# Moving the MLP gradients of an attention backward kernel behind head 29, with their rows in a K/V slot

## The chip, the cores and the metric

The kernel runs on one core of a Trainium2 chip. The metric is the device time of one execution in microseconds (us), given as the median of several runs. The engines are called TensorE (PE in the profile), VectorE (DVE), ScalarE (ACT), GpSimd (POOL) and SyncE (SP; SPq for its queue of instructions). GpSimd and SyncE do little here but issue DMAs.

## The reference

It is one decode step of a transformer block (one token, 32 heads with 8192 cached keys and values of width 128, a gated MLP of width 1728) together with all its gradients:

```python
def _fwd_reference(A_x, A_k_cache, A_v_cache, A_wq, A_wo, B_x, B_w1, B_w3, B_w2):
    # _A_ref: q = x@wq; p = softmax(q k^T * Dh**-0.5); o = p v; o @ wo
    # _B_ref: h = silu(x@w1) * (x@w3); h @ w2
    x = A_x
    xn = _layernorm(x, axis=-1)
    return x + _A_ref(xn, ...) + _B_ref(xn, B_w1, B_w3, B_w2)

def reference(..., grad_out):
    _out, _vjp = jax.vjp(_f, A_x, A_k_cache, A_v_cache, A_wq, A_wo, B_w1, B_w3, B_w2)
    return (_out, *_vjp(grad_out))
```

The gradients of K and V are outer products, one per head, each as large as the cache that was read: a head loads 4.2 MB and stores 4.2 MB. The gradients of W1, W3 and W2 are outer products too, 6.6 MB in all. Their inputs are known early, so they can be written at any time. The change is about when.

## The kernel before

All K and V tiles, and the large gradient tiles, take turns in nine slots of 2 MB. A new tile gets the slot that is released next, and whoever touches it first waits for the slot's last user, which is mostly a store that has to land.

```python
    kvpool = ctx.enter_context(tc.tile_pool(name="kv", bufs=9))
    def kv_tile(nm):
        return kvpool.tile([P, KVN], BF16, name=nm, tag="kv")
    def load_kv(n):                        # in the order K0, V0, K1, V1, ...
        for h, w in kv_seq[kv_next[0]:kv_next[0] + n]:
            t = kv_tile("Vt" if w else "Kt")
            nc.sync.dma_start(t[:], (vc if w else kc)[h])
            kv_tiles[h, w] = t
        kv_next[0] += n
```

A head has three parts. `phase_a(h)` transposes K on TensorE in eight pieces, each copied out by ScalarE (`KT`), makes the scores, and does the softmax (VectorE: `mrow`, `gmax`, `negM`; ScalarE: `E`). `phase_t(h)` makes the gradient of the softmax from V (VectorE: `T`, `negD`, `U`; TensorE sums `T` into `dp`). `phase_b(h)` overwrites V and K by their gradients on VectorE and stores them. Each engine runs its instructions in the order of the program that the compiler made; an instruction that waits holds everything behind it on its engine (ScalarE stands 12.13 us in this way in after, and 17.11 us in e5, both shown below).

The MLP gradients need two "broadcast rows", vectors of 1728 elements repeated on all 128 partitions. They are made by a chain between ScalarE and TensorE:

```python
    def make_bc(wi, bc, on_act):
        for b0 in range(0, NB, 4):                      # four steps for a row
            dg = small.tile([P, 4, P], BF16, name="dgm", tag="dg", bufs=1)
            ... nc.scalar.activation(dg[:, k, :], ident_bf[:], ACTF.Copy, scale=dgu[...])
            pb = pst_f()
            nc.tensor.matmul(pb[:, 0:bn * P], lhsT=ones_bf[:], rhs=dg[...], ...)
            nc.scalar.copy(bc[:, f0:f1], pb[:, 0:f1 - f0])   # L420 in the profile
        return bc

    def grads_bc(wi):                                   # into a spare weight buffer
        t = wpool.tile([P, NC * GW], BF16, name="bc_t", tag=("wo_g", "wq_g")[wi], bufs=3)
        gt["bc", wi] = make_bc(wi, t, True)

    def grads_w(wi):                                    # gradient of W1, W3
        t = kv_tile("oW")
        ...
        if wi == 0:
            gt["C"] = kv_tile("oC")
        ...                                             # 5 multiplies on VectorE, 2 stores
    def grads_w2():                                     # gradient of W2
        t = kv_tile("oD")
        ...                                             # 14 multiplies on VectorE, 3 stores
```

The main loop (H is 32):

```python
    for h in range(2, H):
        ...
        if h == H - 6:
            grads_bc(0)
            grads_bc(1)
        if h + 1 < H:
            phase_a(h + 1)
            phase_t(h + 1)
        ...
        phase_b(h)
        if h == H - 6:
            grads_w(0)
        elif h == H - 5:
            grads_w(1)
        elif h == H - 4:
            grads_w2()
        load_kv(2)
```

So in the kernel before, three gradient tiles enter the rotation ahead of the last loads: `oW` and `oC` before V30 and K31, and the second `oW` before V31. `oD` comes after all loads.

Of the kernel before, what the change touches and what calls it, by code (L numbers as in the profile page):

```python
# [9 lines left out]
BF16 = mybir.dt.bfloat16  # L10
F32 = mybir.dt.float32
ALU = mybir.AluOpType
# [4 lines left out]
P = 128  # L17
# [4 lines left out]
def kernel(  # L22
# [22 lines left out]
    nc = tc.nc  # L45
    H = A_k_cache.shape[1]
    SK = A_k_cache.shape[2]
    DH = A_k_cache.shape[3]
    D = A_x.shape[2]
    F = B_w1.shape[1]  # L50
    assert DH == P and D % P == 0 and SK % P == 0
    NC = D // P
# [3 lines left out]
    GW = GH * DH  # L56
    KVN = J * DH
# [4 lines left out]
    wpool = ctx.enter_context(tc.tile_pool(name="wp", bufs=2))  # L62
# [9 lines left out]
    dkc = out_2.rearrange("b h (p j) d -> (b h) p (j d)", p=P)  # L72
    dvc = out_3.rearrange("b h (p j) d -> (b h) p (j d)", p=P)
# [12 lines left out]
    g_bc = consts.tile([P, D], BF16, name="g_bc")  # L86
    nc.scalar.dma_start(g_bc[:], grad_out.rearrange("a b d -> (a b d)").partition_broadcast(P))

    NB = (F + P - 1) // P
    NFULL = F // P  # L90
    RB = F - NFULL * P
    NBA = 12
    NA = NC - 1

    def kv_tile(nm):
        return kvpool.tile([P, KVN], BF16, name=nm, tag="kv")
# [12 lines left out]
    def load_group(g):  # L109
        wq_g = wpool.tile([P, NC, GW], BF16, name="wq_g", tag="wq_g", bufs=3)  # L110
        nc.sync.dma_start(wq_g[:], wq_v[:, :, g * GW:(g + 1) * GW])
        wo_g = wpool.tile([P, GH, D], BF16, name="wo_g", tag="wo_g", bufs=3)
        nc.sync.dma_start(wo_g[:], wo_v[:, g * GH:(g + 1) * GH, :])
        grp[g] = dict(wq=wq_g, wo=wo_g)
# [5 lines left out]
    def load_kv(n):  # L120
# [5 lines that stand above are left out]
# [49 lines left out]
    def pst_f():  # L175
        return ps_t.tile([P, 512], F32, name="pF", tag="pT")
# [7 lines left out]
    xn_col = consts.tile([P, NC], F32, name="xn_col")  # L184
# [147 lines left out]
    def outer(dst, vec, pair, lo, hi):  # L332
        n = hi - lo
        nc.vector.tensor_tensor(  # L334
            dst[:, lo * DH:hi * DH].rearrange("p (j a b) -> p j a b", a=DH // 2, b=2),
            vec.rearrange("p (a b) -> p a b", b=2).unsqueeze(1).to_broadcast([P, n, DH // 2, 2]),
            pair[:, lo:hi, :].unsqueeze(2).to_broadcast([P, n, DH // 2, 2]), ALU.mult)

    def phase_b(h):
        g, hh = divmod(h, GH)  # L340
        G_ = grp[g]
        qh = G_["qs"][:, hh, :]
        doh = G_["do"][:, hh, :]
        Vt = kv_tiles.pop((h, 1))
        Kt = kv_tiles.pop((h, 0))
        S_ = hd.pop(h)
        P2, U2 = S_["P2"], S_["U2"]
        for lo in range(0, J, J // 2):
            outer(Vt, doh, P2, lo, lo + J // 2)
        (nc.sync if h >= H - 2 else nc.gpsimd).dma_start(dvc[h], Vt[:])  # L350
        for lo in range(0, J, J // 2):
            outer(Kt, qh, U2, lo, lo + J // 2)
        (nc.sync if h >= H - 2 else nc.gpsimd).dma_start(dkc[h], Kt[:])  # L353

    def finish_group(g):
        G_ = grp[g]
# [45 lines left out]
    def make_bc(wi, bc, on_act):  # L402
        id2 = ident_bf[:].rearrange("p (a b) -> p a b", b=2)
        for b0 in range(0, NB, 4):
            bn = min(4, NB - b0)
            dg = small.tile([P, 4, P], BF16, name="dgm", tag="dg", bufs=1)
            if on_act:
                for k in range(bn):
                    nc.scalar.activation(dg[:, k, :], ident_bf[:], ACTF.Copy, scale=dgu[:, wi, b0 + k:b0 + k + 1])
            else:  # L410
                nc.vector.tensor_tensor(dg[:, 0:bn].rearrange("p k (a b) -> p k a b", b=2),
                                        id2.unsqueeze(1).to_broadcast([P, bn, P // 2, 2]),
                                        dgu2[:, wi, b0:b0 + bn, :].unsqueeze(2).to_broadcast([P, bn, P // 2, 2]),
                                        ALU.mult)
            pb = pst_f()
            nc.tensor.matmul(pb[:, 0:bn * P], lhsT=ones_bf[:],
                             rhs=dg[:, 0:bn].rearrange("p k a -> p (k a)"), start=True, stop=True)
            f0 = b0 * P
            f1 = min(F, f0 + bn * P)
            nc.scalar.copy(bc[:, f0:f1], pb[:, 0:f1 - f0])  # L420
        return bc

    hcol = consts.tile([P, NB], F32, name="hcol")
# [67 lines left out]
                                     start=False, stop=True, skip_group_check=True)  # L491

    gt = {}

    def grads_bc(wi):
        t = wpool.tile([P, NC * GW], BF16, name="bc_t", tag=("wo_g", "wq_g")[wi], bufs=3)
        gt["bc", wi] = make_bc(wi, t, True)

    def grads_w(wi):
        t = kv_tile("oW")  # L500
        v = t[:, 0:NA * F].rearrange("p (c f) -> p c f", f=F)
        bc = gt["bc", wi]
        if wi == 0:
            gt["C"] = kv_tile("oC")
        tb = gt["C"][:, wi * F:(wi + 1) * F]
        dv = (dw1_v, dw3_v)[wi]
        for ci in range(NA):
            nc.vector.tensor_scalar(v[:, ci, :], bc[:, 0:F], xn_col[:, ci:ci + 1], None, ALU.mult)
        nc.gpsimd.dma_start(dv[:, 0:NA, :], v)
        nc.vector.tensor_scalar(tb, bc[:, 0:F], xn_col[:, NA:NC], None, ALU.mult)  # L510
        nc.gpsimd.dma_start(dv[:, NA, :], tb)

    def grads_w2():
        t = kv_tile("oD")
        d2a = t[:, 0:NBA * D].rearrange("p (b c) -> p b c", c=D)
        d2b = gt["C"][:, 2 * F:2 * F + (NB - NBA) * D].rearrange("p (b c) -> p b c", c=D)
        for b in range(NBA, NB):
            nc.vector.tensor_scalar(d2b[:, b - NBA, :], g_bc[:], hcol[:, b:b + 1], None, ALU.mult)
        nc.gpsimd.dma_start(out_8[NBA * P:NFULL * P, :].rearrange("(fb p) c -> p fb c", p=P),
                            d2b[:, 0:NFULL - NBA, :])  # L520
        if RB:
            nc.gpsimd.dma_start(out_8[NFULL * P:F, :], d2b[0:RB, NFULL - NBA, :])
        for b in range(NBA):
            nc.vector.tensor_scalar(d2a[:, b, :], g_bc[:], hcol[:, b:b + 1], None, ALU.mult)
        nc.gpsimd.dma_start(out_8[0:NBA * P, :].rearrange("(fb p) c -> p fb c", p=P), d2a)


    prep_group(0)
    for h in range(2):
        phase_a(h)  # L530
        phase_t(h)
        phase_b(h)
        load_kv(2)
        if h == 0:
            load_group(1)
# [4 lines left out]
    for h in range(2, H):  # L540
        g, hh = divmod(h, GH)
        if hh == 1 and g + 1 < NG:
            load_group(g + 1)
        if hh == GH - 1 and g + 1 < NG:
            prep_group(g + 1)
        if h == H - 6:
            grads_bc(0)
            grads_bc(1)
        if h + 1 < H:
            phase_a(h + 1)  # L550
            phase_t(h + 1)
        if h == H - 1:
            finish_group(g)
        phase_b(h)
        if h == H - 6:
            grads_w(0)
        elif h == H - 5:
            grads_w(1)
        elif h == H - 4:
            grads_w2()  # L560
        load_kv(2)
        if hh == GH - 1 and h < H - 1:
            finish_group(g)
# [58 lines left out]
```

## Time and profile before

| | |
|---|---|
| time, median of 4 runs in the comparison | 753.07 us (751.85 to 754.21) |
| bytes moved, mean rate in the profiled run | 304.35 MB, 405 GB/s |
| TensorE, VectorE busy | 592.9 us (79%), 549.3 us (73%) |
| mean granted TensorE clock | 0.776 |
| last K/V load issued | 691.46 us |
| head 31's scores complete (`mrow`) | 712.76 us |

The first view is three lines of the page: the span in 40 slices of 18.8 us, with the DMA's busy share in tenths and its rate, and the packet counts.

```profile
DMA  8999999999999999999999999999999999799978
GB/s 343 388 425 430 412 427 413 419 419 381 424 421 423 419 412 411 417 421 416 427 430 424 427 423 430 425 414 420 421 433 384 394 363 428 294 356 424 412 299 345
DMA packets 35051, 304.35 MB, mean 405 GB/s; under 512 B 2840, under 2 KB 13912, under 8 KB 18568
```

The rate drops from about 420 GB/s to 294 and 356 in slices 35 and 36, and to 299 in slice 39. The next view reads these stretches in windows of 10 us. Its columns are the busy time of each engine (number of instructions), the granted TensorE clock, the DMA share and the rate.

```profile
core 0: us, PE busy (x) PEld busy (x) DVE busy (x) ACT busy (x) POOL busy (x), PEclk, DMA share, GB/s
640.00:650.00 10.00, 4.09 (x99) 4.09 (x99) 5.07 (x8) 1.59 (x3) 0.76 (x1) 0.50 0.75 319
650.00:660.00 10.00, 7.72 (x81) 5.98 (x79) 7.70 (x9) 2.92 (x5) 1.08 (x2) 0.80 0.62 223
...
720.00:730.00 10.00, 2.79 (x77) 2.39 (x75) 9.26 (x12) 0.00 (x0) 0.00 (x0) 0.78 0.47 197
```

There are two holes: 640 to 660 us (319 and 223 GB/s), and 720 to 730 us (197 GB/s). The first is explained by the queue of SyncE, which issues the loads. This is the line for the gradient tiles in the list of what it waited for between 560 us and the end (us in total, times, longest; the other lines are cut).

```profile
SPq L123 <- DMA out_dram<-oW: 40.8, 2, 22.8
```

SyncE stood 40.8 us, in two waits, for the gradient tiles' own stores (`oW`) to land before it could load into their slots. These are the last three loads in SyncE's timeline (start, duration, engine, line, operation):

```profile
658.48 0.33 SPq L123 DMA_DIRECT2D Vt<-in_A_v_cache_dram  x1
672.95 0.33 SPq L123 DMA_DIRECT2D Kt<-in_A_k_cache_dram  x1
691.46 0.33 SPq L123 DMA_DIRECT2D Vt<-in_A_v_cache_dram  x1
```

These are V30, K31 and V31; the two waits end at V30 and V31. K31 follows 14.5 us after V30 without a wait for `oW`. VectorE met the same slots from the other side, as its timeline shows; in brackets is its idle time before the instruction and what ended it.

```profile
644.93 0.67 DVE L508 TENSOR_SCALAR oW<-bc_t,xn_col 128x1728 bf16<-128x1728 bf16 x1 [11.11 <-DMA out_dram<-Vt]
645.51 0.34 DVE L324 SCALAR_TENSOR_TENSOR U<-DP,negD,P 128x128 bf16<-128x128 f32 x1
```

VectorE stood 11.11 us at the first `oW` multiply for a Vt store, and head 27's `U`, on which its K store depends, stood behind it.

The broadcast rows are visible in ScalarE's timeline at head 26:

```profile
597.50 0.59 ACT L420 CAST bc_t<-pF 128x512 bf16<-128x512 f32 x1 [2.90 <-PE sA L319]
...
617.23 1.01 ACT L265 COPY KT<-pT 128x1024 bf16<-128x1024 bf16 x1 [0.53 <-PE pT L261]
```

From 597.5 to 617.2 us ScalarE copies no `KT`: the chain of eight row copies (L420), of which the first is shown with the `KT` copy that follows the last, keeps the place.

### The profile page before, as it was taken

The numbers are of one execution on the slowest core, as the hardware profiler recorded it, in microseconds if no ns is written. First come the engines' busy times: TensorE is split into PE (matmuls) and PEld (weight loads), VectorE is DVE, ScalarE is ACT, GpSimd is POOL, SyncE is SP. The second block draws the span as 40 slices with busy tenths as digits, with TensorE's granted clock in tenths as the row PEclk, the third lists the DMA queues.
The fourth block names the chain that finished last, engine by engine and source line by source line (L and its number), as shares of the span: only waits on it lengthen the run. The fifth ranks groups of instructions, "written<-read, shape, count | busy, mean of one in ns | idle before, by whom it ended". The sixth has DMA issues, their size and how long they took to land.

```text
span 751.9 us, 23383 instructions
## 1 busy us (share of the span) xinstructions
PE 592.9 (79%) x10618; PEld 506.5 (67%) x10637; DVE 549.3 (73%) x802; ACT 331.1 (44%) x480; POOL 52.3 (7%) x91
## 2 busy tenths in 40 slices
PE   5978899898869868799768994799637978679852
PEld 3855687887668757787667873688527857568741
DVE  1787777787779738986788674986549793588895
ACT  3801555544528414554427451455504666236401
POOL 0000000100001000100001000100001000011101
PEclk9965998798769859797759696797856958668665
DMA  8999999999999999999999999999999999799978
GB/s 343 388 425 430 412 427 413 419 419 381 424 421 423 419 412 411 417 421 416 427 430 424 427 423 430 425 414 420 421 433 384 394 363 428 294 356 424 412 299 345
DMA packets 35051, 304.35 MB, mean 405 GB/s; under 512 B 2840, under 2 KB 13912, under 8 KB 18568
## 3 DMA queue, kind: packets, MB, share of 16 engines
q1 hardware_dynamic: 22404, 159.74, 52.0%
q0 software_dynamic: 12384, 142.96, 45.4%
q8 instruction: 83, 1.36, 0.7%
q10 hardware_dynamic: 164, 0.17, 0.1%
q14 instruction: 16, 0.13, 0.0%
HBM read 151.51 MB, written 151.34 MB: 403 GB/s over the span
## 4 chain that ended last, share of the span: by engine, by line
issue 43%; PE 23%; DMA 10%; DVE 7%; POOL 3%; ACT 2%; POOLq 0%; SPq 0%; ACTq 0%
PE dp L308 6%; PE pT L261 6%; DMA wo_g<-in_A_wo_dram 4%; DVE Kt L334 4%; DMA out_dram<-Vt 3%; DMA wq_g<-in_A_wq_dram 3%; PE sA L327 2%; PE sA L290 2%; PE sA L268 2%; ACT KT L265 2%; DVE Vt L334 1%; POOL out_dram L353 1%; POOL out_dram L350 1%; PE pT L381 1%; PE acc L490 1%
## 5 line engine op out<-in xcount | busy, mean ns | idle before, releaser
L265 ACT COPY KT<-pT 128x1024 bf16<-128x1024 bf16 x256 | 243.6, 1038 | 53.9 <-PE pT L261 52.7
L308 PE MATMUL dp<-T,ident_bf 128*128 128x256 bf16 x1024 | 182.0, 312 | 32.4 <-DVE T L306 31.1
L306 DVE TENSOR_TENSOR T<-Vt,do_g 128x2048 bf16<-128x2048 bf16 x128 | 154.2, 1214 | 51.5 <-DMA Vt<-in_A_v_cache_dram 43.9
L261 PE MATMUL pT<-ident_bf,Kt 128*128 128x128 bf16 x2048 | 174.3, 236 | 1.7 <-issue 1.5
L334 DVE TENSOR_TENSOR Vt<-do_g,P 128x4096 bf16<-128x4096 bf16 x64 | 146.0, 2282 | 3.6 <-PE sA L290 3.6
L334 DVE TENSOR_TENSOR Kt<-qs_g,U 128x4096 bf16<-128x4096 bf16 x64 | 145.5, 2279 | 2.0 <-PE sA L327 1.9
L261 PEld LDWEIGHTS <-Kt 128*128 128x128 bf16 x2048 | 138.0, 107 | 6.3 <-issue 3.5
L308 PEld LDWEIGHTS <-ident_bf 128*128 128x128 bf16 x1024 | 103.2, 111 | 57.3 <-issue 36.3
L268 PEld LDWEIGHTS <-KT 128*128 128x128 bf16 x2048 | 81.8, 99 | 33.8 <-ACT KT L265 23.5
L268 PE MATMUL sA<-qc_g,KT 128*128 128x1 bf16 x2048 | 90.4, 165 | 15.3 <-ACT KT L265 8.2
L327 PE MATMUL sA<-U,Kt 128*128 128x1 bf16 x2048 | 58.4, 164 | 33.2 <-DVE U L324 31.7
L327 PEld LDWEIGHTS <-Kt 128*128 128x128 bf16 x2048 | 58.7, 101 | 35.1 <-issue 34.5
L290 PEld LDWEIGHTS <-Vt 128*128 128x128 bf16 x2048 | 56.7, 97 | 19.7 <-issue 18.4
L290 PE MATMUL sA<-P,Vt 128*128 128x1 bf16 x2048 | 56.5, 164 | 13.8 <-DVE P L287 13.6
L329 ACT COPY od_g<-sA 128x2 f32<-128x2 f32 x32 | 5.1, 160 | 129.1 <-PE sA L327 94.9
L281 ACT ACTIVATE E<-sA,negM 128x64 f32<-128x64 f32 x32 | 10.4, 325 | 100.9 <-DVE negM L278 100.9
L350 POOL DMA_DIRECT2D out_dram<-Vt x30 | 16.4, 548 | 407.8 <-DVE junk L318 228.3
L235 ACT COPY KT<-pT 128x1024 bf16<-128x1024 bf16 (+1 forms) x24 | 20.0, 874 | 33.4 <-PE pT L233 33.2
L353 POOL DMA_DIRECT2D out_dram<-Kt x30 | 16.3, 545 | 167.0 <-DVE U L324 63.9
L274 DVE TENSOR_REDUCE gmax<-sA 1x1 f32<-1x128 f32 x32 | 8.8, 276 | 22.0 <-PE sA L272 21.8
L271 DVE TENSOR_REDUCE mrow<-sA 128x1 f32<-128x64 f32 x32 | 7.1, 221 | 24.2 <-PE sA L268 23.9
L312 DVE TENSOR_REDUCE DP<-dp 128x64 f32<-128x256 f32 x32 | 13.3, 415 | 14.5 <-PE dp L308 14.5
(144 smaller groups left out, 488.2 us busy)
## 6 DMA issues: line engine op xcount, KB each, us to landing
Kt<-in_A_k_cache_dram SPq DMA_DIRECT2D x32, 2048.0 KB, 17.8
Vt<-in_A_v_cache_dram SPq DMA_DIRECT2D x32, 2048.0 KB, 24.4
out_dram<-Vt POOLq DMA_DIRECT2D x30, 2048.0 KB, 15.1
out_dram<-Kt POOLq DMA_DIRECT2D x30, 2048.0 KB, 19.9
wq_g<-in_A_wq_dram SPq DMA_DIRECT2D x8, 640.0 KB, 24.6
wo_g<-in_A_wo_dram SPq DMA_DIRECT2D x8, 640.0 KB, 25.4
out_dram<-wo_g POOLq DMA_DIRECT2D x8, 640.0 KB, 20.4
out_dram<-wq_g POOLq DMA_DIRECT2D x8, 640.0 KB, 23.8
```

What stands on the lines that cost most here:

```text
L235: nc.scalar.copy(wT[:, 0:len(bl), :], pT[:, 0:len(bl), :])
L261: ins = nc.tensor.transpose(pT[:, k, :], K3[:, 8 * c + k, :], ident_bf[:])
L265: nc.scalar.copy(KT[:], pT[:])
L268: nc.tensor.matmul(sA[:, j:j + 1], lhsT=KT[:, k, :], rhs=qcol, start=(j == 0), stop=True, skip_group_check=True)
L290: nc.tensor.matmul(sA[:, OC:OC + 1], lhsT=V3[:, j, :], rhs=P2[:, j, 0:1], start=False, stop=(j == J - 1), skip_group_check=True)
L306: nc.vector.tensor_tensor(T3, V3[:, :, ds_], do_h[:, ds_].unsqueeze(1).to_broadcast([P, J, QD]), ALU.mult)
L308: ins = nc.tensor.matmul(dp[:], lhsT=ident_bf[:], rhs=T3[:, :, R * i:R * (i + 1)], start=(q == 0 and i == 0), stop=(q == DH // QD - 1 and ...
L312: nc.vector.tensor_reduce(DP[:], dp[:], AX.X, ALU.add)
L327: nc.tensor.matmul(sA[:, OC + 1:OC + 2], lhsT=K3[:, j, :], rhs=U2[:, j, 0:1], start=False, stop=(j == J - 1), skip_group_check=True)
L334: nc.vector.tensor_tensor(dst[:, lo * DH:hi * DH].rearrange("p (j a b) -> p j a b", a=DH // 2, b=2), vec.rearrange("p (a b) -> p a b", b=2 ...
L350: (nc.sync if h >= H - 2 else nc.gpsimd).dma_start(dvc[h], Vt[:])
L353: (nc.sync if h >= H - 2 else nc.gpsimd).dma_start(dkc[h], Kt[:])
```

## The change

The intent was to let the last loads go ahead of all gradient tiles, and to make and store the gradients next to head 29's outer products, where the DMA would otherwise run out of work. The rows move from spare weight buffers into a third K/V slot (`oC`), the W2 gradient into weight buffers, and the gradient stores from GpSimd's queue to SyncE's. Head 30's own two stores go the other way, from SyncE to GpSimd.

```diff
-        (nc.sync if h >= H - 2 else nc.gpsimd).dma_start(dvc[h], Vt[:])
+        (nc.sync if h >= H - 1 else nc.gpsimd).dma_start(dvc[h], Vt[:])
 ... (the same for dkc)
-    def grads_bc(wi):
-        t = wpool.tile([P, NC * GW], BF16, name="bc_t", tag=("wo_g", "wq_g")[wi], bufs=3)
-        gt["bc", wi] = make_bc(wi, t, True)
+    CB = 2 * F + (NB - NBA) * D
 ...
+    def grads_bc():
+        gt["C"] = kv_tile("oC")
+        for wi in range(2):
+            gt["bc", wi] = make_bc(wi, gt["C"][:, CB + wi * F:CB + (wi + 1) * F], True)
 ... (grads_w: nc.gpsimd.dma_start -> nc.sync.dma_start)
     def grads_w2():
-        t = kv_tile("oD")
 ...
+        for i, b0 in enumerate(range(0, NBA, 4)):
+            t = wpool.tile([P, 4, D], BF16, name="oD", tag=("wo_g", "wq_g")[i % 2], bufs=3)
+            for k in range(4):
+                nc.vector.tensor_scalar(t[:, k, :], g_bc[:], hcol[:, b0 + k:b0 + k + 1], None, ALU.mult)
+            nc.sync.dma_start(out_8[b0 * P:(b0 + 4) * P, :].rearrange("(fb p) c -> p fb c", p=P), t[:])
 ... (the last two blocks of W2 into oC, stored on nc.sync)
-        if h == H - 6:
-            grads_bc(0)
-            grads_bc(1)
         if h + 1 < H:
             phase_a(h + 1)
             phase_t(h + 1)
 ...
         phase_b(h)
-        if h == H - 6:
+        if h == H - 4:
+            grads_bc()
+        elif h == H - 3:
             grads_w(0)
-        elif h == H - 5:
             grads_w(1)
-        elif h == H - 4:
             grads_w2()
         load_kv(2)
```

More of the change, by code (lines that the diff above doesn't have):

```diff
@@ L349, in phase_b @@
             outer(Vt, doh, P2, lo, lo + J // 2)
-        (nc.sync if h >= H - 2 else nc.gpsimd).dma_start(dvc[h], Vt[:])
+        (nc.sync if h >= H - 1 else nc.gpsimd).dma_start(dvc[h], Vt[:])
         for lo in range(0, J, J // 2):
             outer(Kt, qh, U2, lo, lo + J // 2)
-        (nc.sync if h >= H - 2 else nc.gpsimd).dma_start(dkc[h], Kt[:])
+        (nc.sync if h >= H - 1 else nc.gpsimd).dma_start(dkc[h], Kt[:])
     def finish_group(g):
@@ L493 @@
     gt = {}
-    def grads_bc(wi):
-        t = wpool.tile([P, NC * GW], BF16, name="bc_t", tag=("wo_g", "wq_g")[wi], bufs=3)
-        gt["bc", wi] = make_bc(wi, t, True)
+    CB = 2 * F + (NB - NBA) * D
+    assert CB + 2 * F <= KVN
+    def grads_bc():
+        gt["C"] = kv_tile("oC")
+        for wi in range(2):
+            gt["bc", wi] = make_bc(wi, gt["C"][:, CB + wi * F:CB + (wi + 1) * F], True)
     def grads_w(wi):
@@ L502, in grads_w @@
         bc = gt["bc", wi]
-        if wi == 0:
-            gt["C"] = kv_tile("oC")
         tb = gt["C"][:, wi * F:(wi + 1) * F]
@@ L507, in grads_w @@
         for ci in range(NA):
-            nc.vector.tensor_scalar(v[:, ci, :], bc[:, 0:F], xn_col[:, ci:ci + 1], None, ALU.mult)
-        nc.gpsimd.dma_start(dv[:, 0:NA, :], v)
-        nc.vector.tensor_scalar(tb, bc[:, 0:F], xn_col[:, NA:NC], None, ALU.mult)
-        nc.gpsimd.dma_start(dv[:, NA, :], tb)
+            nc.vector.tensor_scalar(v[:, ci, :], bc, xn_col[:, ci:ci + 1], None, ALU.mult)
+        nc.sync.dma_start(dv[:, 0:NA, :], v)
+        nc.vector.tensor_scalar(tb, bc, xn_col[:, NA:NC], None, ALU.mult)
+        nc.sync.dma_start(dv[:, NA, :], tb)
     def grads_w2():
-        t = kv_tile("oD")
-        d2a = t[:, 0:NBA * D].rearrange("p (b c) -> p b c", c=D)
-        d2b = gt["C"][:, 2 * F:2 * F + (NB - NBA) * D].rearrange("p (b c) -> p b c", c=D)
+        for i, b0 in enumerate(range(0, NBA, 4)):
[3 more added lines that the diff above has]
+            nc.sync.dma_start(out_8[b0 * P:(b0 + 4) * P, :].rearrange("(fb p) c -> p fb c", p=P), t[:])
+        d2b = gt["C"][:, 2 * F:CB].rearrange("p (b c) -> p b c", c=D)
         for b in range(NBA, NB):
             nc.vector.tensor_scalar(d2b[:, b - NBA, :], g_bc[:], hcol[:, b:b + 1], None, ALU.mult)
-        nc.gpsimd.dma_start(out_8[NBA * P:NFULL * P, :].rearrange("(fb p) c -> p fb c", p=P),
-                            d2b[:, 0:NFULL - NBA, :])
+        nc.sync.dma_start(out_8[NBA * P:NFULL * P, :].rearrange("(fb p) c -> p fb c", p=P),
+                          d2b[:, 0:NFULL - NBA, :])
         if RB:
-            nc.gpsimd.dma_start(out_8[NFULL * P:F, :], d2b[0:RB, NFULL - NBA, :])
-        for b in range(NBA):
-            nc.vector.tensor_scalar(d2a[:, b, :], g_bc[:], hcol[:, b:b + 1], None, ALU.mult)
-        nc.gpsimd.dma_start(out_8[0:NBA * P, :].rearrange("(fb p) c -> p fb c", p=P), d2a)
+            nc.sync.dma_start(out_8[NFULL * P:F, :], d2b[0:RB, NFULL - NBA, :])
     prep_group(0)
```

## The prediction

> What bounds the kernel now: DMA, nearly everywhere. The page gives 304.35 MB at a mean of 405 GB/s; its 40 slices show the DMA engines at nine tenths or more in all but five. The Trainium skill ("DMA: Bandwidth & Descriptors", Specifications) states a fabric ceiling of 435 GB/s; the best slice here, 433, agrees. 304.35 MB cost about 718 us at 424 GB/s (an estimate from the 400 to 560 us stretch). The stretch from 560 to 752 us moves only 371 GB/s, a loss of about 24 us.
>
> Where the tail loses (windows, timeline, waits):
> - 640 to 660 us: 319 and 223 GB/s, about 7 us lost. The gradient tiles sit in the K/V rotation before the last three loads. VectorE stands 11.1 us at the first oW multiply, waiting for a Vt store to land (644.9), and head 27's U and stores stand behind it. SyncE's queue waits 40.8 us for oW's own stores before it can load V30 (658.5) and V31 (691.5).
> - 720 to 730 us: 197 GB/s, about 5 us lost. V31 came late, nothing is left to store, and from 712.8 to 741.7 VectorE is busy without a break: head 31's products, the outer products of heads 30 and 31, the last group's gradients. Then an 8.2 us store.
> - 597 to 616 us: making the broadcast rows is a chain of ScalarE and TensorE during which no transposes are made.
>
> What the change does. No bytes and no arithmetic go. The last three loads no longer queue behind gradient tiles: V30 can start near 645 instead of 658, K31 near 654 instead of 673, V31 near 660 instead of 691 (when V26, K26, V27 land). The 11 us wait goes. The 6.6 MB of gradient stores (about 16 us of DMA) come after all loads, where a head stores only 4.2 MB per some 18 us of compute, and fill that hole. VectorE's gradient work (10 multiplies of 0.66 us, 14 of about 0.37: 12 us) stands next to head 30's scores, where VectorE would wait for TensorE. The broadcast chain of some 16 us moves from head 26 to before head 30's transposes: gained early, paid late.
>
> Two bounds for the end. DMA: 39.7 MB remain at 640 us; at 420 mixed and 394 store-only (the rate of 726 to 750) they take until 738 to 740. Compute: TensorE needs 592.9/32 = 18.5 us a head; head 31's scores should be ready near 702 instead of 712.8, and the 39 us after them remain: 741.
>
> Predicted: 741 us; 734 to 749 holds it 8 times in 10. Faster by over 2% (below 737.8) 0.27, within 2% 0.72, slower 0.01.
>
> Right if: the hole at 640 to 660 is gone (over 390 GB/s); no VectorE wait over 3 us before oW; the last K/V load is issued 20 us or more earlier; SyncE's queue shows no wait for oW's stores; the mean rate is about 411; bytes are the same; VectorE's unbroken final run starts about 10 us earlier.
>
> Wrong if: ScalarE stands at the first broadcast copy, waiting for K27's store, and holds head 30's transposes (over 745); VectorE waits for head 28's stores before oW; a lower granted clock slows TensorE in a denser tail; or the DMA keeps a hole of 5 us before V30's store. Better if heads 26 and 27, freed of the chain, fill the DMA before 640 too: 733 to 737.

## The result and the profile after

| | before | after |
|---|---|---|
| median of 4 runs, us | 753.07 (751.85 to 754.21) | 755.01 (753.3 to 755.23) |
| profiled span, us | 751.9 | 753.1 |
| mean rate, GB/s | 405 | 404 |
| mean granted TensorE clock | 0.776 | 0.769 |
| last K/V load issued, us | 691.46 | 665.27 |
| head 31's scores complete, us | 712.76 | 715.01 |

The ratio of after to before is 1.0021, with a 95% interval from 0.9999 to 1.0043. A ratio is the mean time of one kernel's runs over that of the other's runs of the same rounds, so it is not quite the ratio of the medians in the table. No gain came, and the predicted range of 734 to 749 us did not hold the time.

First the rates and the packet counts of the page, of after:

```profile
GB/s 345 385 427 427 415 426 425 414 400 401 425 425 423 412 430 423 420 424 421 428 427 426 420 423 430 411 385 394 425 429 427 421 395 352 427 424 227 390 293 343
DMA packets 37019, 304.35 MB, mean 404 GB/s; under 512 B 2872, under 2 KB 15672, under 8 KB 20536
```

The bytes are the same. The slices with 294 and 356 GB/s now show 427 and 424, but the next one shows 227, where before had 424. The windows of after, with the same columns as before:

```profile
640.00:650.00 10.00, 4.01 (x137) 3.85 (x137) 9.99 (x18) 0.00 (x1) 1.06 (x2) 0.73 1.01 431
650.00:660.00 10.00, 10.00 (x167) 9.27 (x165) 9.65 (x14) 8.81 (x13) 1.63 (x2) 0.76 1.00 420
670.00:680.00 10.00, 1.81 (x6) 1.02 (x6) 1.30 (x2) 3.89 (x13) 0.00 (x0) 0.50 1.02 434
680.00:690.00 10.00, 9.69 (x115) 7.08 (x116) 6.64 (x11) 5.11 (x15) 0.00 (x0) 0.55 0.46 196
690.00:700.00 10.00, 8.45 (x169) 7.50 (x167) 10.00 (x10) 8.45 (x16) 1.52 (x2) 0.83 0.63 264
720.00:730.00 10.00, 3.58 (x81) 3.10 (x80) 9.84 (x11) 0.00 (x0) 0.53 (x1) 0.83 0.55 216
```

Before had in the two windows from 680 us:

```profile
680.00:690.00 10.00, 8.89 (x178) 7.76 (x177) 9.90 (x17) 8.18 (x11) 2.26 (x4) 1.00 1.02 420
690.00:700.00 10.00, 9.58 (x157) 7.66 (x155) 7.42 (x17) 0.57 (x3) 0.84 (x2) 0.66 1.01 419
```

The hole at 640 to 660 us is gone (431 and 420 GB/s). A new one stands at 680 to 700 us (196 and 264), and the old one at 720 to 730 us stayed (216). A smaller dip at 620 to 630 us (287 GB/s, 435 in before) is not explained by any run here. In 670 to 680 us TensorE is busy for 1.81 us and VectorE for 1.30 of 10.

SyncE's last three loads did come early, as intended. Here is its timeline:

```profile
644.96 0.33 SPq L123 DMA_DIRECT2D Vt<-in_A_v_cache_dram  x1
655.07 0.33 SPq L123 DMA_DIRECT2D Kt<-in_A_k_cache_dram  x1
665.27 0.33 SPq L123 DMA_DIRECT2D Vt<-in_A_v_cache_dram  x1
```

V31 was issued at 665.27 us, 26 us earlier than before. Its slot had held V27, whose store was issued at 643.48 and landed 21.7 us later, at 665.2. The next slot to come free is that of K27, and it goes to `oC`, where the rows are to be written. These are GpSimd's issues of three stores (V27, K27 and V29; the last store before V29's, K28's, was issued at 666.48), then the trace's answer for K27's store alone, with its time from issue to landing:

```profile
643.48 0.53 POOL L350 DMA_DIRECT2D out_dram<-Vt  x1 [13.12 <-DVE junk L318]
648.09 0.53 POOL L353 DMA_DIRECT2D out_dram<-Kt  x1 [4.08 <-DVE U L324]
...
692.80 0.53 POOL L350 DMA_DIRECT2D out_dram<-Vt  x1 [25.77 <-DVE Vt L334]
```

```profile
L353 POOL DMA_DIRECT2D out_dram<-Kt x1: 532/532/532, 648.1 to 648.1; - x1
...
DMA to landing us min/median/max: 26.8/26.8/26.8
```

So K27's slot came free at 648.09 + 26.8 = 674.9 us. Now ScalarE's timeline:

```profile
662.16 0.75 ACT L409 ACTIVATE dgm<-ident_bf,dgu 128x128 bf16<-128x128 bf16 x2
675.05 0.58 ACT L420 CAST oC<-pF 128x512 bf16<-128x512 f32 x1 [12.13 <-issue]
...
693.34 0.32 ACT L420 CAST oC<-pF 128x192 bf16<-128x192 f32 x1 [0.46 <-PE pF L416]
694.19 10.18 ACT L265 COPY KT<-pT 128x1024 bf16<-128x1024 bf16 x11 [0.54 <-PE pT L261]
```

At 662.9 us ScalarE reaches the first row copy into `oC` and stands 12.13 us, until 675.05 us. The profile writes "issue" because it saw nobody release it; 674.9 us is where K27's store landed. Then the chain of rows runs to 693.7 us, and head 30's `KT` copies begin only at 694.19. What stood behind the wait shows on TensorE and VectorE:

```profile
663.38 0.27 PE L272 MATMUL sA<-ident_f,mrow 128*1 128x128 f32 x1
676.86 0.59 PE L416 MATMUL pF<-dgm,ones_bf 128*128 128x512 bf16 x1 [13.21 <-ACT dgm L409]
677.37 0.58 PE L275 MATMUL sA<-gmax,negones_f 1*128 1x1 f32 x2
```

```profile
677.99 0.16 DVE L278 COPY negM<-sA 128x1 f32<-128x1 f32 x1 [11.83 <-PE sA L275]
```

TensorE had its `mrow` transpose of head 29 at 663.38 us, but its next instruction in order is the row chain's second matmul, and that waits 13.21 us for the `dgm` that ScalarE makes after its copy. The matmul L275, which gives `negM` of head 29's softmax, stands behind it, and VectorE waits 11.83 us for that. Head 29's V store goes out at 692.80 us, after a gap of 26 us without a store by GpSimd. The new hole in the DMA lies in that gap: V31's load landed at 679.8 us, V28's store at 687.0, and K28's at 692.3.

The gain of the earlier loads was there up to head 29 and was gone after the wait and the chain; e1 and e2 below test which of them cost it. It can be followed by the times at which each head's scores were complete:

| head | 27 | 28 | 29 | 30 | 31 |
|---|---|---|---|---|---|
| before, us | 627.85 | 655.04 | 683.38 | 691.59 | 712.76 |
| after, us | 610.18 | 633.26 | 663.10 | 702.07 | 715.01 |

After leads by 18 to 22 us up to head 29, then lies 10 us behind at head 30. From head 31's scores on, both kernels take the same 38 to 39 us.

### The profile page after: what moved, and what is told of

Same layout as the page of the kernel before. It is cut to its first block, busy times and chain, and to the rows that moved or that the text cites. A ratio compares the mean times of both kernels' runs of the same rounds, so it can differ in the third digit from the quotient of the medians.

```text
span 753.1 us, 23390 instructions
## 1 busy us (share of the span) xinstructions
PE 595.5 (79%) x10617; PEld 508.1 (67%) x10637; DVE 548.9 (73%) x802; ACT 331.1 (44%) x480; POOL 48.8 (6%) x86
## 4 chain that ended last, share of the span: by engine, by line
issue 44%; PE 19%; DMA 14%; DVE 6%; ACT 3%; POOL 3%; POOLq 0%; SPq 0%; ACTq 0%
PE dp L308 5%; DMA out_dram<-Kt 4%; PE pT L261 4%; DMA wo_g<-in_A_wo_dram 4%; DMA Kt<-in_A_k_cache_dram 3%; DMA wq_g<-in_A_wq_dram 3%; DVE Kt L334 3%; PE sA L327 2%; ACT KT L265 2%; PE sA L290 2%; DVE Vt L334 2%; PE sA L268 2%; POOL out_dram L350 1%; POOL out_dram L353 1%; PE pT L381 1%
## 5 line engine op out<-in xcount | busy, mean ns | idle before, releaser
L275 PEld LDWEIGHTS sA<-gmax,negones_f 1*128 1x128 f32 x64 | 11.8, 229 | 21.4 <-issue 16.8
```

Source lines behind the costliest of these rows:

```text
L275: nc.tensor.matmul(sA[:, J + P:J + P + 1], lhsT=negones_f[0:1, :], rhs=gmax[0:1, 0:1], start=False, stop=True, skip_group_check=True)
```

## The experiments

The kernel before was run beside each set, on the same chip; its medians there were 753.43, 753.58, 753.42 and 753.58 us (7 runs each). All other entries have 4 runs. All were correct but e7. Intervals that leave out 1 tell a difference.

| label | what | median us | ratio to before, 95% interval |
|---|---|---|---|
| (after) | the change | 755.01 | 1.0021 (0.9999 to 1.0043) |
| e1_rows_early | rows at head 26, weight buffers | 747.6 | 0.9922 (0.9906 to 0.9938) |
| e2_rows_late_spare | rows where after has them, weight buffers | 748.28 | 0.9928 (0.9911 to 0.9944) |
| e3_stores_pool | after, gradient stores on GpSimd | 755.22 | 1.0028 (1.0002 to 1.0055) |
| e4_rows_once | rows of the MLP stage kept | 752.17 | 0.998 (0.995 to 1.001) |
| e5_w2_scalar | e1, part of W2 on ScalarE | 758.3 | 1.0056 (1.003 to 1.0082) |
| e6_mult_twice | e1, gradient multiplies doubled | 750.6 | 0.9966 (0.9936 to 0.9996) |
| e7_half_fold | e1, less TensorE work (wrong result) | 747.34 | 0.9916 (0.9897 to 0.9936) |
| e8_e1_stores_pool | e1, gradient stores on GpSimd | 751.58 | 0.9973 (0.9924 to 1.0022) |
| e9_w1_first | e1, W1 multiplies before the outer products | 747.11 | 0.9916 (0.9891 to 0.994) |
| e10_w1_first_w2_scalar | e9, part of W2 on ScalarE | 747.35 | 0.9919 (0.989 to 0.9949) |
| e11_small_pool | e1, two small stores on GpSimd | 748.08 | 0.9931 (0.9909 to 0.9953) |
| e12_w1_first_small_pool | e10, two small stores on GpSimd | 748.37 | 0.9923 (0.9892 to 0.9953) |

### The wait and the place of the rows: e1 and e2

The theory was that the wait of ScalarE for K27's slot cost the gain. Both kernels take that wait away: the rows go into weight buffers again, and `oC` is taken only with the gradients. In e2 the chain stays where after has it. In e1 it also moves back to head 26, as in before.

```diff
 # e2, from after (e1 has the calls at h == H - 6, ahead of phase_a(h + 1))
-    def grads_bc():
-        gt["C"] = kv_tile("oC")
-        for wi in range(2):
-            gt["bc", wi] = make_bc(wi, gt["C"][:, CB + wi * F:CB + (wi + 1) * F], True)
+    def grads_bc(wi):
+        t = wpool.tile([P, NC * GW], BF16, name="bc_t", tag=("wo_g", "wq_g")[wi], bufs=3)
+        gt["bc", wi] = make_bc(wi, t, True)[:, 0:F]
 ... (grads_w(0): gt["C"] = kv_tile("oC"))
         if h == H - 4:
-            grads_bc()
+            grads_bc(0)
+            grads_bc(1)
```

> The changed kernel with one part undone: the broadcast rows are made at head 26 again, in the weight buffers, as before; the K/V order, the three slots and the SyncE stores of the change stay. Theory S (in the changed kernel ScalarE stands 12 us in order at the first row copy for head 27's Kt store, and head 29's softmax behind it, and the row chain of some 18 us then runs on the compute path): both go, so 738 to 744 us, ratio to the kernel before 0.98 to 0.99; no ScalarE wait over 3 us before a row copy. Rival R (the tail is bounded by DMA and a throttled TensorE, whatever the order): 751 to 757. Rival Q (the SyncE queue of small packets is what costs): 751 to 757 as well.

> The changed kernel with the rows still made at head 28, but in weight buffers long free instead of the third K/V slot. This takes away the wait for the slot alone and keeps the late chain. Theory S with the wait as the main cost: about 743 us (12 us less than the changed kernel). Theory S with the chain's place as the main cost: 748 to 755. Rival R and rival Q: 753 to 757.

Measured: e2 748.28 us, 6.7 us less than after; e1 747.6 us, 7.4 us less. In e2 ScalarE's timeline has the chain in the same place (its first and last copies are shown), without the wait:

```profile
666.44 0.58 ACT L420 CAST bc_t<-pF 128x512 bf16<-128x512 f32 x1 [0.46 <-PE pF L416]
...
684.87 0.32 ACT L420 CAST bc_t<-pF 128x192 bf16<-128x192 f32 x1 [0.36 <-PE pF L416]
685.60 10.26 ACT L265 COPY KT<-pT 128x1024 bf16<-128x1024 bf16 x11 [0.42 <-PE pT L261]
```

The first row copy waits 0.46 us instead of 12.13. The chain ends at 685.2 us and head 30's `KT` copies start at 685.60, 8.6 us before after's. The wait is shown to cost about 7 us. (In e2 the gradient tiles also take the freed slots in another order, `oW` before `oC`.) Both medians are above what was expected for the wait as the main cost, 743 for e2 and 738 to 744 for e1; e2's lies at the edge of the range given for the chain's place, but moving the chain back as well, in e1, gained no more. The medians of e1 and e2 differ by 0.7 us and their intervals overlap, so the place of the chain is not separated in the time. In the profiles it moves things: head 31's scores are complete at 702.05 us in e1, at 710.46 in e2, where VectorE also stood 4.86 us at the second `oW` for a K store.

### The store queue: e3 and e8

The rival was that the gradient stores, now on SyncE's queue, cost the gain. Both kernels put them back on GpSimd's queue, e3 in after, e8 in e1.

```diff
-        nc.sync.dma_start(dv[:, 0:NA, :], v)
+        nc.gpsimd.dma_start(dv[:, 0:NA, :], v)
 ... (all gradient stores)
```

> The changed kernel with its gradient stores back on the GpSimd queue, nothing else. Theory S: the 12 us ScalarE wait and the chain stay, 753 to 758 us. Rival Q: 5 us or more faster than the changed kernel, below 750.

> e1_rows_early with its gradient stores on the GpSimd queue instead of SyncE's. In e1_rows_early SyncE's V31 and K31 stores land 13 and 12 us after issue, behind gradient stores on the same queue. If that queue is what holds the end: 743 to 745. If the shared DMA engines are (theory D, the DMA drains what came too late): 746 to 749, no change beyond 1 us.

Measured: e3 755.22 us, like after, with ScalarE standing 16.24 us at its first row copy; e8 751.58 us, with two runs near 748.5 and two near 754.6, which is outside both ranges expected. e3 also confirms who ends the wait: there K27's store was issued at 644.45 us and landed 30.5 us later, at 674.95, and the row copy started at 675.10. SyncE's queue did not eat the gain, and on top of e1 it is the better place if there is a difference. This agrees with the Trainium skill, "Trainium Kernel Development and Optimization", Key Constraints, by which DMAs from all issuing engines run on the same 16 DMA engines and only the issue time is saved: e3 and after differ by 0.2 us. The issue time was not always small, though: in e8 GpSimd took 7.62 us to issue one `oW` store. Head 30's own stores were put back in no run; what their move did is not shown.

### Making no second chain: e4

The MLP stage at the start makes the same rows once. This kernel keeps them in one of the three weight buffers of each kind to the end, so that no chain is made in the tail and two buffers are left for the weights.

```diff
-            bc = make_bc(wi, t_tile(), False)
+            bc = make_bc(wi, wpool.tile([P, NC * GW], BF16, name="bc_t", tag=("wo_g", "wq_g")[wi], bufs=3), False)
+            gt["bc", wi] = bc[:, 0:F]
```

> The changed kernel with the rows not made a second time: those made in the MLP stage are kept to the end in one of the three weight buffers of each kind. No row chain at all in the tail. Theory S: the lowest of the four, 735 to 741 us, if the group loads do not suffer from two buffers. Rival R: 750 to 757. If the two buffers delay weight loads, waits of SyncE for the weight stores will show it.

Measured: 752.17 us, 4.6 us above e1. The chain is gone, but the last group's weights, loaded at 513.99 us in after, could be loaded only at 600.02 us, and the heads fell behind: head 31's scores were complete at 708.41 us, 6.4 us later than in e1. So this kernel lost more than the chain cost; that the late weights are the reason fits these times, but no run tests it alone.

### Part of W2 on ScalarE: e5, an accidental repetition of the wait

To shorten VectorE's block in e1, eight of the fourteen W2 multiplies go to ScalarE ahead of `phase_b(29)`.

```diff
+                nc.scalar.activation(t[:, k, :], g_bc[:], ACTF.Copy, scale=hcol[:, b0 + k:b0 + k + 1])
 ...
+        if h == H - 3:
+            w2_piece(0, True)
+            w2_piece(1, True)
```

> e1_rows_early with 8 of the 14 W2 multiplies moved to ScalarE, next to head 29, and their two stores placed ahead of the other gradient stores. Theory D (what keeps e1_rows_early 6 us above the prediction: VectorE makes all gradients in one block of 10 us before head 31's softmax, and their stores come too late to fill a hole of the DMA at 680 to 700 us, some 5 us): the hole shrinks, the block shortens by 2.4 us, total 742 to 745. Rival T (TensorE, slowed by a lower granted clock in a denser tail, sets the pace): 746 to 749, no gain.

Measured: 758.3 us, 10.7 us slower than e1. The expected gain did not come, because the compiler put the first of these right behind head 29's copies. One line of ScalarE's timeline, then one of VectorE's:

```profile
680.88 1.55 ACT L520 ACTIVATE oD<-g_bc,hcol 128x640 bf16<-128x640 bf16 x2 [17.11 <-DMA out_dram<-wo_g]
```

```profile
684.34 0.28 DVE L274 TENSOR_REDUCE gmax<-sA 1x1 f32<-1x128 f32 x1 [18.25 <-PE sA L272]
```

ScalarE waits 17.11 us for the store of group 6's `wo_g` (issued at 650.2 us, landed 30.5 us later) to free the buffer, and VectorE's `gmax` of head 29 waits 18.25 us behind it. Another slot, another instruction, the same mechanism: ScalarE, first in the path of the next softmax, touches a buffer whose store has not landed. This shows again what such a wait costs in this place.

### What holds e1 at 747.6 us: e6, e7, e9, e10

e1 is still 6.6 us above the prediction. Head 31's scores are complete at 702.05 us, and the last multiply of K31 is done at 731.8 us. The prediction had 702 for the scores, but for a kernel with the chain late; e2, which has that, reached 710.46, so this agreement is luck. The windows of e1:

```profile
680.00:690.00 10.00, 10.00 (x177) 9.66 (x175) 6.69 (x10) 5.03 (x6) 0.53 (x1) 0.50 0.69 284
690.00:700.00 10.00, 4.01 (x121) 3.72 (x119) 10.00 (x20) 3.01 (x5) 0.67 (x1) 0.67 0.81 333
...
740.00:742.00 2.00, 0.00 (x0) 0.00 (x0) 0.00 (x0) 0.00 (x0) 0.00 (x0) 0.50 0.18 73
742.00:744.00 2.00, 0.00 (x0) 0.00 (x0) 0.00 (x0) 0.00 (x0) 0.00 (x0) 0.50 0.06 25
```

The gradients are one VectorE block from 692.12 to 702.05 us; before it the DMA runs short (284 and 333 GB/s). From 742 us to 744 the DMA share is 0.06, that of one engine of 16, with 25 GB/s: one engine moves data alone.

e6 does each gradient multiply twice. e7 leaves out half of the matmuls that sum `T` into `dp` in heads 27 to 31. e9 makes the four large W1 multiplies and their store ahead of head 29's outer products. e10 adds eight W2 multiplies on ScalarE, tied behind head 31's last `KT` copy so that e5's wait cannot come back, and puts the other six behind head 31's softmax chain.

```diff
 # e6
+            for _ in range(2):
                 nc.vector.tensor_scalar(v[:, ci, :], bc, xn_col[:, ci:ci + 1], None, ALU.mult)
 # e7
+            NI = QD // R if h < H - 5 else QD // R // 2
-            for i in range(QD // R):
+            for i in range(NI):
 # e9
+        if h == H - 3:
+            grads_wa(0)          # ahead of phase_b(h)
 # e10, beside e9's
+                tc.add_manual_dep(ins.ins, last_kt[-1].ins.name, NOSYNC, ...)
```

> e1_rows_early with each of the 24 gradient multiplies on VectorE done twice, the result unchanged, 10 us more VectorE work. Theory D (the block lies on the path to the last stores): 755 to 758, nearly the whole 10 us. What the prediction said (the multiplies stand where VectorE waits for TensorE): 747 to 750.

> e1_rows_early with half of the fold matmuls into dp left out in heads 27 to 31 (a wrong result on purpose), some 3 to 5 us of TensorE less per head, all else the same. Rival T: 735 to 741. Theory D: 744 to 748, a small gain at most.

> e1_rows_early with the four large W1 multiplies and their 1.7 MB store placed ahead of head 29's outer products. Theory D: the hole of the DMA at 680 to 700 us shrinks by some 4 us; the same VectorE work in all; 743 to 746. If the block of VectorE alone is the bound: no change, 746 to 749.

> e9_w1_first, and 8 of the 14 W2 multiplies on ScalarE, this time ordered after head 31's last copy so that ScalarE does not stand at a buffer (in e5_w2_scalar it stood 17 us), the rest after head 31's softmax. VectorE's block before that softmax shortens by some 7 us. Both bounds lowered: 740 to 745.

Measured: about 10 us more VectorE work cost only 3.0 us (e6, just above the 747 to 750 expected if the work fits into waits). Less work gained nothing: e7 finished VectorE at 728.4 us instead of 731.8 and took 747.34 us, which also refutes TensorE's pace as the limit of e1; e9 took 747.11 us, having met a wait of 5.5 us for K28's store at the second `oW`; e10 finished VectorE at 727.5 us and took 747.35, where 740 to 745 was expected. In e7, K31's store was issued at 728.5 us and took 15.9 us to land, in e1 12.2 us from 731.9. Finishing sooner only made the last stores take longer to land; in e7 one DMA engine alone was still moving data from 740 to 744 us (25 GB/s).

### The one late DMA engine: e11 and e12

In e1, between 719 and 730 us, packets of 1280 bytes (the end of W2's gradient) trickled at one or two a microsecond. The theory was that they, taken in turns with 16 KB packets of GpSimd's queue, held up one engine.

```diff
-        nc.sync.dma_start(out_8[NBA * P:NFULL * P, :]...
+        nc.gpsimd.dma_start(out_8[NBA * P:NFULL * P, :]...
-            nc.sync.dma_start(out_8[NFULL * P:F, :], d2b[0:RB, NFULL - NBA, :])
+            nc.gpsimd.dma_start(out_8[NFULL * P:F, :], d2b[0:RB, NFULL - NBA, :])
```

> The rows made at head 26, with the last two W2 gradient stores (160 and 80 KB, packets of 1280 bytes) moved from SyncE's queue to GpSimd's. In that kernel, after 717 us, these 1280-byte packets trickled at one or two a microsecond for 13 us, and at the end one DMA engine alone still moved packets of 16 KB and 4 KB for about 4 us. Theory small: the small packets, taken in turns with GpSimd's 16 KB packets, hold up one engine's part of the stores of V31 and K31 behind them on SyncE's queue; then the lone engine at the end goes (last two 2 us slices not below 100 GB/s before the last) and the time falls by 2 to 4 us, to 743.5 to 745.5. Rival: that engine simply has more to do or was late for another reason, and the small packets are only where it shows; then the lone engine stays and the time is 746.5 to 748.5.

> The same change on top of the version with the W1 multiplies first and part of W2 on ScalarE, whose products were done at 727.5 us, 4.3 us earlier, and whose last 5.4 us were one engine's eight 16 KB packets; there SyncE's issues of these two stores took 11.4 and 4.0 us and V31's store was issued only at 724.9. Theory small: the lone engine goes and V31's store is issued before 722; the time falls by 4 to 6 us, to 741.5 to 743.5. Rival: the lone engine stays and the time is 746 to 748.

Measured: 748.08 and 748.37 us, no gain. SyncE did issue V31's store earlier in e11 (722.95 us instead of 725.00), but the lone engine stayed, as a window of e11 shows (742 to 744 us has 25 GB/s as well):

```profile
740.00:742.00 2.00, 0.00 (x0) 0.00 (x0) 0.00 (x0) 0.00 (x0) 0.00 (x0) 0.50 0.06 27
```

The theory of the small packets is refuted. What makes that engine late stays open. At the end of the run its lateness shows in e1, e7 and e9 to e12, and not in before and after, which have a long hole at 720 to 730 us in which an engine could catch up. But the lack of a hole does not explain it: e4's profile has none after 710 us either (no 2 us window below 343 GB/s from 710 to 746), and its DMA ends without a lone engine. And after has a lone engine too, though not at its end: in its hole, from 686 to 688 us, the share is 0.06 with 25 GB/s, and K28's store landed only at 692.3 us. The Trainium skill, "DMA: Bandwidth & Descriptors", Latency and other measured facts, says that DMA engines 7 and 15 are usually slower in traces. It speaks of two engines where these windows show one, and the traces give a packet no engine number, so no run here shows it.

## Why the prediction was wrong

- **What bounds the kernel: right.** The DMA is nine tenths busy or more up to 640 us in both profiles, but for the first slice. The ceiling of 435 GB/s that the prediction took from the Trainium skill ("DMA: Bandwidth & Descriptors", Specifications) agrees with the best slices, 433 GB/s before and 430 after.
- **The first hole goes: right.** 431 and 420 GB/s at 640 to 660 us, no VectorE wait before `oW`, no SyncE wait for `oW`'s stores, V31's load 26 us earlier, the bytes the same.
- **"Gained early, paid late": wrong, the step that failed.** The sum put the broadcast chain at nothing and let head 31's scores be ready "near 702". They came at 715.01 us. The chain in its new place was preceded by a wait of 12.13 us for K27's store, in front of head 29's softmax and head 30's transposes. The prediction had named this wait under "wrong if", with "over 745", but no term of the sum priced it. When V27's and K27's stores would land could have been asked of the profile: the page gave a median of 19.9 us for K stores, and this one, with the loads that the change itself had moved forward beside it, took 26.8 us (30.5 in e3); that these loads made it longer is not tested. e2 shows that the wait alone is worth 6.7 us of the 14 us miss. Without the wait the late chain still kept head 31's scores to 710.46 us (e2), 8.4 us behind e1, so "near 702" fails on the chain too, though the times of e1 and e2 are not separated. And what was "gained early" at head 26 did not last: after led e1 by 13 us at head 27, but only by 3 us at head 29 (663.10 against 665.96). What took the lead away is not shown; no engine is seen waiting for V29's load, which was issued at 624.5 us in after and 624.9 in e1.
- **The 39 us after head 31's scores: mis-sized.** Without the wait and with the chain early (e1) the scores came at 702.05 us, but the end took 44 us instead of 39. The prediction had carried over 39 us from before, where the last stores came after an almost idle stretch of the DMA: the 720 to 730 us window moved 197 GB/s, and K31's store landed in 9.1 us. In e1 the 6.6 MB of gradient stores fill that hole, K31's store lands in 12.2 us, and one DMA engine alone runs on. The prediction filled the hole and kept the short drain; the runs did not show both together. e7 and e10, with the products done 3 to 4 us sooner and no gain in time, show that the drain (the time until the last stores have landed) and no longer VectorE sets the end. The prediction's other bound, the DMA done by 738 to 740 us, missed this too, since it reckoned with 16 engines that end together: in e7 and e11 all but one had ended by about 740 us.
- **A mean rate of about 411: wrong** (404), with the new hole at 680 to 700 us and the old one at 720 to 730. **The unbroken final VectorE run 10 us earlier: wrong** in after (715 to 742.1 us; before 712.8 to 741.7), right in e1 (702.05 to 731.8 us).
- **A lower granted clock** (0.769 against 0.776) is not the cause: e1 had 0.745 and was faster.

## What to carry to other kernels

When a tile moves into a rotating buffer, work out which tile held that slot before and when its store lands under the load of the new schedule; the wait belongs to the first instruction that touches the buffer and holds everything behind it on that engine. Write to a buffer that has been free for long, as e1, e2 and e9 do (747.1 to 748.3 us, 0.7 to 0.8% faster than before). To put such an instruction behind the work that others wait for is the other way; e10 did it for its W2 multiplies, which then did not wait, but no run tried it for the rows. A drain time that was measured beside a hole in the DMA must not be carried over to a schedule that fills the hole.

## What the Trainium skill lacked or had wrong

- "DMA: Bandwidth & Descriptors", Anatomy of one DMA, gives the time of one DMA from GpSimd's queue as 2.0 us plus its bytes over 436 GB/s, which is 6.8 us for a store of 2 MB (an estimate from that page). The trace of after agrees when the DMA has room: V30's store, issued at 725.54 us, landed in 6.6 us. Under load the same size took 21.7 us (V27) and 26.8 us (K27), and a 640 KB store in e5 30.5 us. The page has no figure for a store among many other transfers.
- "DMA: Bandwidth & Descriptors", Where 436 GB/s comes from, says that the HBM side, about 358 GB/s, binds transfers between HBM and SBUF. In before this core moved 403 GB/s of reads and writes over the whole span. The section Measured of the same page has 425 GB/s for a single core and gives 358 to a core only when both cores of a pair stream; the passage that says "binds" lacks this condition. These runs used one core.
- "DMA: Bandwidth & Descriptors", SWDGE vs HWDGE vs iDMA, does not say that the queue changes what the profile counts as packets. The W2 gradient went out as packets of 5120 bytes from GpSimd's queue (before, e3) and as 1280 bytes from SyncE's (after, e1); packets under 2 KB rose from 13912 to 15672.
- No page says that at the end of a dense stretch one DMA engine can run on alone for some microseconds (25 GB/s from 742 to 744 us in e1, 25 to 27 from 740 to 744 in e7 and e11, 25 from 686 to 688 in after). The remark on engines 7 and 15 that is told above is the nearest, and no run here tests it.
